# Joining the quadrant matmuls of x into one run per batch, with shared tail banks

## The chip, the cores and the metric

The kernel runs on one core of one Trainium2 chip. Times are device microseconds (us) of one execution. A kernel's time is the median of its runs. All runs were at a granted TensorE clock of 0.998 to 1.000 of full speed.

TensorE (PE) multiplies; its weights are loaded by separate instructions (PEld). VectorE (DVE) and ScalarE (ACT) read the results out of PSUM, in which this kernel keeps eight tiles of 512 float columns; they are called banks here.

## The reference, cut to what matters

```python
# q, k, v: 8 batches, 8 heads, 576 positions, 64 per head
q_s = softmax(q, axis=-1)
k_s = softmax(k, axis=2)                       # over the positions
kv  = einsum('bhsd,bhse->bhde', k_s, v)        # 64 x 64 per head
x   = einsum('bhsd,bhde->bhse', q_s, kv)       # -> 4608 tokens x 512
out = (silu(x @ w_gate) * (x @ w_val)) @ w_out # 512 -> 1536 -> 512
```

Nearly all arithmetic is in the last line. `kv` and `x` are small, but they use only part of the 128x128 array.

## The kernel before: the parts that matter

Each batch is handled in two groups of four heads (`G` is 0 or 1). `kv` has 64 rows and 128 columns of weights; `x` has 64x64, so four matmuls, one on each quadrant of the array, run together. A quadrant run has a first piece of five position tiles (320 columns) and a tail of four (256 columns), because a bank holds 512 float columns.

```python
BANKS = ((0, 5), (5, 9))

def x(b, G, piece, eng=nc.scalar):
    s = st[b, G]
    t0, t1 = piece
    n = 64 * (t1 - t0)
    xp = [f_tile("xp") for _ in range(2)]            # two banks, one for each h
    for g in range(2):
        for h in range(2):
            r = slice(64 * h, 64 * h + 64)
            nc.tensor.matmul(
                out=xp[h][64 * g:64 * g + 64, 0:n].rearrange("p (t c) -> p t c", c=64),
                lhsT=s["kn"][r, g, :], rhs=s["qt"][g][r, t0:t1, :],
                start=True, stop=True)
    c0 = b * S + 64 * t0
    copy(eng, xt[:, 2 * G, c0:c0 + n], xp[0][:, 0:n])
    nc.vector.tensor_copy(out=xt[:, 2 * G + 1, c0:c0 + n], in_=xp[1][:, 0:n])

def x_both(b, G, eng=nc.scalar):
    for piece in BANKS:
        x(b, G, piece, eng)
    st.pop((b, G))

def kv_pair(b):                                      # both groups: 36 matmuls, 4 banks
    kv(b, 0)
    kv(b, 1)
    for G in range(NG):
        kn_recip(b, G)
        kn(b, G, 1, nc.vector)
        kn(b, G, 0, nc.vector)
# ... (cut)
for ci, (c0, n) in enumerate(chunks):                # 448 tokens, then 512 each
    b = ci + 2
    # ... (cut)
    if ci == 0:
        steps = {2: lambda: kv_kn(2, 0, True), 4: lambda: x_both(2, 0),
                 7: lambda: kv_kn(2, 1, True), 10: lambda: x_both(2, 1)}
    elif b < B:
        steps = {8: lambda: kv_pair(b), 9: lambda: x_both(b, 0),
                 10: lambda: x_both(b, 1)}
    for m in range(MT):                              # 12 "rows" of 128 hidden units
        # ... (cut: at rows 3 and 7 the exponentials of batch b and the w_out matmuls)
        m_unit(c0, n, m)                             # g_ps, u_ps: 8 full-array matmuls
        if m in steps:
            steps[m]()
```

A *row* below is one `m_unit`: four matmuls into `g_ps`, four into `u_ps`, then the SiLU on ACT and the product on DVE, which read the two banks. A *round* is one set of `kv` or `x` matmuls that run together: four quadrants for `x`, two halves for `kv`. A *visit* is an unbroken run of rounds between full-array matmuls. `kn` is `kv` after normalisation, written back as the weights of `x`. A *chunk* is the 448 or 512 tokens that twelve rows work on. `f_tile` hands out the eight PSUM banks in turn; a bank comes free when its last reader is done.

The softmax here doesn't subtract the row's maximum and nothing guards it: scores larger than these inputs give would overflow.

Of the kernel before, what the change touches and what calls it, by code (L numbers as in the profile page):

```python
# [15 lines left out]
def kernel(  # L16
# [19 lines left out]
    nc = tc.nc  # L36

    B, H, S, D = q.shape
# [6 lines left out]
    NG = H // 4  # L45
# [10 lines left out]
    def f_tile(name):  # L56
        return psp.tile([128, 512], FP32, tag="ps", name=name)
# [4 lines left out]
    xt = const.tile([128, KT, n_tok], BF16, name="xt", tag="xt")  # L62
# [39 lines left out]
    def copy(eng, out, in_):  # L102
        if eng is nc.scalar:
            nc.scalar.copy(out=out, in_=in_)  # L104
        else:
            eng.tensor_copy(out=out, in_=in_)  # L106


    st = {}
    BANKS = ((0, 5), (5, 9))  # L110

    def exp(b, G, what):
        s = st.setdefault((b, G), {"vb": vbs[G]})
        s["e" + what] = at.tile([128, T, 2, 64], BF16, tag="e" + what, name="e" + what)
        nc.scalar.activation(  # L115
            out=s["e" + what],
            in_=raw[what, b, G].rearrange("p h (t d) -> p t h d", d=64),
            func=AF.Exp,
        )
# [58 lines left out]
    def kv(b, G):  # L178
        s = st[b, G]
        s["kv"] = [f_tile("kv") for _ in range(2)]  # L180
        for t in range(T):
            for g in range(2):
                r = slice(64 * g, 64 * g + 64)
                nc.tensor.matmul(  # L184
                    out=s["kv"][g][:, 0:129],
                    lhsT=s["ek"][r, t, :, :].rearrange("p h d -> p (h d)"),
                    rhs=s["vb"][r, t, 0:129],
                    start=(t == 0),
                    stop=(t == T - 1),
                )  # L190

    def kn_recip(b, G):
        s = st[b, G]
        s["kvr"] = at.tile([128, 2], FP32, tag="kvr", name="kvr")
        for g in (1, 0):
            nc.vector.reciprocal(out=s["kvr"][:, g:g + 1], in_=s["kv"][g][:, 128:129])
# [13 lines left out]
# [4 lines that stand above are left out]
        xp = [f_tile("xp") for _ in range(2)]  # L214
# [5 lines that stand above are left out]
                    lhsT=s["kn"][r, g, :],  # L220
                    rhs=s["qt"][g][r, t0:t1, :],
                    start=True, stop=True,
# [9 lines that stand above are left out]
# [8 lines left out]
    def kv_kn(b, G, split=False):  # L240
        kv(b, G)
        kn_recip(b, G)
        kn(b, G, 1, nc.scalar if split else nc.vector)
        kn(b, G, 0, nc.vector)

    def warm_up(n):
        ps = f_tile("warm_ps")
        for _ in range(n):
            nc.tensor.matmul(  # L249
                out=ps[:, 0:256], lhsT=zero[:, 0:128], rhs=zero, start=True, stop=True  # L250
            )

    def kv_pair(b):
        kv(b, 0)
        kv(b, 1)
# [4 lines that stand above are left out]
# [64 lines left out]


    make_identity(nc, ident)
    A, Z = BANKS
    with tc.manual_schedule():
        for G in range(NG):
            load(0, G, "q", q)  # L330
        for G in range(NG):
            load(0, G, "k", k)
            load(0, G, "v", v)
        warm = const.tile([128, 1], FP32, name="warm", tag="warm")
        nc.vector.memset(warm, 0.0)
        nc.scalar.activation(out=warm, in_=warm, func=AF.Exp)
        zero = const.tile([128, 256], BF16, name="zero", tag="zero")
        nc.vector.memset(zero, 0.0)  # L338
        for vb in vbs:
            nc.vector.memset(vb[:, :, 128:129], 1.0)  # L340

        exp(0, 0, "q")
        exp(0, 1, "q")
        norm_sum(0, 0)
        norm_mul(0, 0, nc.gpsimd)
        norm_sum(0, 1)
        norm_mul(0, 1, nc.vector)
        exp(0, 0, "k")
        cast_v(0, 0, nc.scalar)

        w_dma = []
        for c0, n in ((0, 256), (256, 256), (512, 512), (1024, 512)):
            w_dma.append(w_slice(wg, moe_w_gate, c0, n))
            w_dma.append(w_slice(wv, moe_w_val, c0, n))
        tc.add_manual_dep(w_dma[0].ins, dmas["v", 0, 0].ins.name, SYNC, reason="order of loads")
        for m0 in (0, 4, 8):
            w_dma.append(wo_slice(m0, 4))

        warm_up(WARM[0])
        for G in range(NG):  # L360
            for piece in BANKS:
                tr(0, G, piece, nc.vector)
        exp(0, 1, "k")
        kv(0, 0)
        kn_recip(0, 0)
        kn(0, 0, 1, nc.scalar)
        kn(0, 0, 0, nc.vector)
        cast_v(0, 1, nc.vector, *A)
        cast_v(0, 1, nc.scalar, *Z)
        warm_up(WARM[1])  # L370
        x(0, 0, A)
        x(0, 0, Z)
        kv(0, 1)
        kn_recip(0, 1)
        kn(0, 1, 1, nc.scalar)
        kn(0, 1, 0, nc.vector)
        warm_up(WARM[2])
        x(0, 1, A)
        x(0, 1, Z)

        load(1, 0, "q", q, after=w_dma[-3])
        load(1, 1, "q", q)
        for G in range(NG):
            load(1, G, "k", k)
            load(1, G, "v", v)
        load_group(2, 0)

        for m in range(MT):
            m_unit(0, S, m)

        exp(1, 0, "q")
        exp(1, 1, "q")
        exp(1, 0, "k")
        cast_v(1, 0, nc.gpsimd)
        cast_v(1, 1, nc.gpsimd)
        load_group(2, 1)
        o_unit(0, nc.scalar)
        norm(1, 0)
        o_unit(1, nc.scalar)
        exp(1, 1, "k")  # L400
        norm(1, 1)
        o_unit(2, nc.scalar)
        for piece in BANKS:
            tr(1, 0, piece, nc.vector)
        kv_kn(1, 0, split=True)
        for piece in BANKS:
            tr(1, 1, piece, nc.vector)
        exp(2, 0, "q")

        def between():  # L410
            kv_kn(1, 1, split=True)
            x_both(1, 0, nc.vector)

        finish = o_unit(3, between=between)
        exp(2, 0, "k")
        x_both(1, 1)
        finish()
        norm(2, 0)
        tr_dma(2, 0)
        cast_v(2, 0, nc.gpsimd)  # L420
        cast_v(2, 1, nc.gpsimd)
        exp(2, 1, "q")
        exp(2, 1, "k")

        chunks = [(S, 448)] + [(c, 512) for c in range(1024, n_tok, 512)]
        for ci, (c0, n) in enumerate(chunks):
            b = ci + 2
            first_o = 4 * ci
            final = ci == len(chunks) - 1
            steps = {}  # L430
            if ci == 0:
                steps = {2: lambda: kv_kn(2, 0, True), 4: lambda: x_both(2, 0),
                         7: lambda: kv_kn(2, 1, True), 10: lambda: x_both(2, 1)}
            elif b < B:
                steps = {8: lambda: kv_pair(b), 9: lambda: x_both(b, 0),
                         10: lambda: x_both(b, 1)}
            for m in range(MT):
                if ci == 0 and m == 4:
                    norm_sum(2, 1)
                    norm_mul(2, 1, nc.gpsimd)  # L440
                    tr_dma(2, 1)
                    load_group(3, 0)
                    load_group(3, 1)
                if ci > 0 and m in (3, 7):
                    if b < B:
                        att_head(b, m // 4)
                        if m == 7 and b + 1 < B:
                            load_group(b + 1, 0)
                            load_group(b + 1, 1)
                    o_unit(first_o + (0 if m == 3 else 2))  # L450
                    if not (final and m == 7):
                        o_unit(first_o + (1 if m == 3 else 3))
                m_unit(c0, n, m)
                if m in steps:
                    steps[m]()
        o_unit(first_o + 3)
        last = n_tok // 128 - 4
        for j in range(last, last + 3):
            o_unit(j)
        o_last(last + 3)  # L460
# [30 lines left out]
```

## Time and profile before

| | before |
|---|---|
| time, median of the first 3 runs (6 in all) | 319.42 us (319.35 us) |
| span of the profiled run | 317.4 us |
| PE busy | 310.4 us |
| PE waits, all | 1.7 us |

From the page of the kernel before: the span, the busy line (us, share of the span, instructions), and the chain of work that ended last.

```profile
span 317.4 us, 5037 instructions
...
PE 310.4 (98%) x1920; PEld 157.1 (50%) x1948; DVE 175.5 (55%) x332; ACT 149.2 (47%) x224; POOL 31.1 (10%) x33
...
PE 82%; DMA 10%; DVE 3%; POOL 2%; ACT 1%; issue 1%; SPq 0%; DVEq 0%; ACTq 0%
```

PE is the chain. A few matmul records are missing (1920 of 1948), which changes no start that is read below. The waits of PE in the kernel before (who waited for whom, us in total, times, longest):

```profile
PE warm_ps L249 <- DVE zero L338: 1.1, 1, 1.1
PE tp L160 <- DVE qs L140: 0.4, 1, 0.4
PE kv L184 <- DVE vb L106: 0.2, 1, 0.2
```

All three belong to the start. The list misses one place: it counts from a matmul's modelled end, and so hides short waits. By single starts, the first four `g_ps` matmuls of chunk 0 come about 0.6 us late in all, while batch 1's x is being read out (the last cast on DVE ends at 54.56 us, the fourth `g_ps` starts at 54.61 us). Apart from these, the feed-forward part shows no wait to take away; what is left is PE's own instruction stream. That stream around batch 3, from the timeline of PE in the kernel before (start us, us, engine, line, operation, tiles, form, count):

```profile
132.96 1.03 PE L270 MATMUL u_ps<-xt,wv 128*128 128x512 bf16 x4
133.92 1.22 PE L184 MATMUL kv<-vb,ek 64*128 64x129 bf16 x36
135.07 1.04 PE L270 MATMUL g_ps<-xt,wg 128*128 128x512 bf16 x4
135.94 1.03 PE L270 MATMUL u_ps<-xt,wv 128*128 128x512 bf16 x3
136.90 0.44 PE L218 MATMUL xp<-qtd,kn 64*64 64x320 bf16 x8
137.27 1.04 PE L270 MATMUL g_ps<-xt,wg 128*128 128x512 bf16 x4
138.15 1.03 PE L270 MATMUL u_ps<-xt,wv 128*128 128x512 bf16 x4
139.10 0.44 PE L218 MATMUL xp<-qtd,kn 64*64 64x320 bf16 x8
139.47 1.04 PE L270 MATMUL g_ps<-xt,wg 128*128 128x512 bf16 x4
```

One must read the starts here. The durations (379 ns for 512 columns) have modelled ends and overlap the next matmul, which starts 216 ns later, so they show no gap anywhere. A row takes 1.73 us undisturbed (eight starts, 216 ns apart). From the `g_ps` at 137.27 to that at 139.47 it takes 2.20 us: the x visit in between costs 0.47 us. The single records of the first visit (start in us, distance to the last matmul start before) split that:

```
136.591         u_ps, full array, 512 columns
136.900  0.309  xp, first of four quadrants, 320 columns (others 3 to 4 ns apart)
137.060  0.150  xp, first of four quadrants, 256 columns
137.271  0.201  g_ps, full array            (0.201 after the last quadrant's start)
137.498  0.227  g_ps, full array
137.714  0.216  g_ps, full array
```

Evictions of x in the kernel before, groups with different shapes kept apart (count, then busy us and mean ns, then idle time before):

```profile
L226 DVE CAST xt<-xp 128x320 bf16<-128x320 f32 x16 | 7.7, 484 | 0.5 <-PE xp L218 0.5
L226 DVE CAST xt<-xp 128x256 bf16<-128x256 f32 x16 | 6.6, 415 | 0.0
L104 ACT CAST xt<-xp 128x320 bf16<-128x320 f32 x15 | 6.4, 425 | 6.6 <-PE xp L218 6.6
L104 ACT CAST xt<-xp 128x256 bf16<-128x256 f32 x15 | 5.7, 378 | 0.0
```

### The profile page before, as it was taken

How to read it: one execution, taken by the hardware profiler on the slowest of the kernel's cores; microseconds unless marked ns; L12 is line 12 of the kernel's file. 1: busy time of each engine (PE TensorE's matmuls, PEld its weight loads, DVE VectorE, ACT ScalarE, POOL GpSimd, SP SyncE). 2: the span in 40 equal slices, each digit the busy share in tenths (PEclk: the TensorE clock that was granted, in tenths of full speed). 3: DMA queues.
4: the chain of work that ended last, by engine and by line, in shares of the span. 5: the costliest groups of instructions: out<-in, count | busy, mean ns of one | idle time of the engine just before them, and what ended most of it. 6: DMA issues, size and time to landing. Idle time of an engine off the chain costs nothing.

```text
span 317.4 us, 5037 instructions
## 1 busy us (share of the span) xinstructions
PE 310.4 (98%) x1920; PEld 157.1 (50%) x1948; DVE 175.5 (55%) x332; ACT 149.2 (47%) x224; POOL 31.1 (10%) x33
## 2 busy tenths in 40 slices
PE   8999999999999999999999999999999999999995
PEld 6777744554445444444444444444444444444444
DVE  2934479964647664774577366746575333333422
ACT  4753387744763475547364547355734122312300
POOL 1930023121100110011001100020000000000000
PEclk9999999999999999999999999999999999999999
DMA  7999999449145905392519440963150213020134
GB/s 269 252 190 206 281 392 393 130 116 367 22 84 153 379 24 103 74 385 94 103 38 355 162 103 1 310 241 64 41 103 2 44 22 67 3 61 5 35 67 99
DMA packets 39176, 46.34 MB, mean 146 GB/s; under 512 B 16368, under 2 KB 22384, under 8 KB 39152
## 3 DMA queue, kind: packets, MB, share of 16 engines
q1 hardware_dynamic: 33104, 41.17, 42.5%
q0 software_dynamic: 5808, 4.72, 9.7%
q8 instruction: 15, 0.25, 0.3%
q10 hardware_dynamic: 240, 0.13, 0.2%
q14 instruction: 9, 0.07, 0.1%
HBM read 37.75 MB, written 9.44 MB: 149 GB/s over the span
## 4 chain that ended last, share of the span: by engine, by line
PE 82%; DMA 10%; DVE 3%; POOL 2%; ACT 1%; issue 1%; SPq 0%; DVEq 0%; ACTq 0%
PE g_ps L270 26%; PE o_ps L297 26%; PE u_ps L270 26%; DMA wo<-in_moe_w_out_dram 5%; PE kv L184 2%; DMA v<-in_v_dram 2%; DMA q<-in_q_dram 2%; PE xp L218 1%; POOL wg L92 1%; POOL wv L92 1%; DVE qs L140 1%; PE o_ps L318 1%; DVE rs L131 1%; DVE xt L226 0%; SPq L77 0%
## 5 line engine op out<-in xcount | busy, mean ns | idle before, releaser
L278 ACT ACTIVATE sg<-g_ps 128x512 bf16<-128x512 f32 (+2 forms) x120 | 64.9, 554 | 132.9 <-PE g_ps L270 126.8
L279 DVE TENSOR_TENSOR hr<-sg,u_ps 128x512 bf16<-128x512 bf16 (+2 forms) x120 | 74.9, 633 | 90.7 <-PE u_ps L270 84.1
L270 PE MATMUL g_ps<-xt,wg 128*128 128x512 bf16 (+2 forms) x469 | 110.3, 358 | 0.7
L270 PE MATMUL u_ps<-xt,wv 128*128 128x512 bf16 (+2 forms) x468 | 109.6, 357 | 0.7
L297 PE MATMUL o_ps<-wo,hr 128*128 128x512 bf16 x415 | 93.3, 379 | 0.3
L270 PEld LDWEIGHTS <-wv 128*128 128x128 bf16 x480 | 46.9, 98 | 46.9 <-issue 0.3
L270 PEld LDWEIGHTS <-wg 128*128 128x128 bf16 x480 | 45.3, 98 | 46.2 <-issue 2.6
L297 PEld LDWEIGHTS <-hr 128*128 128x128 bf16 x420 | 41.0, 98 | 49.1 <-issue 0.2
L106 POOL CAST vb<-v 128x1152 bf16<-128x1152 f32 x14 | 17.8, 1270 | 167.2 <-DMA v<-in_v_dram 115.0
L131 DVE TENSOR_REDUCE rs<-eq 128x18 f32<-128x1152 bf16 x16 | 21.6, 1352 | 21.9 <-ACT eq L115 21.8
L106 DVE COPY o_sb<-o_ps 128x512 f32<-128x512 f32 x32 | 21.1, 686 | 20.6 <-PE o_ps L297 20.6
L140 DVE TENSOR_TENSOR qs<-eq,rr 128x1152 bf16<-128x1152 bf16 x14 | 19.8, 1415 | 0.5
L115 ACT ACTIVATE eq<-q 128x1152 bf16<-128x1152 f32 x16 | 18.5, 1163 | 3.2 <-DMA q<-in_q_dram 3.1
L115 ACT ACTIVATE ek<-k 128x1152 bf16<-128x1152 f32 x16 | 18.4, 1152 | 1.3 <-DMA k<-in_k_dram 1.3
L278 ACT ACT_TABLE_LOAD x12 | 15.4, 1283 | 0.2
L208 DVE TENSOR_SCALAR kn<-kv,kvr 64x64 bf16<-64x64 f32 x52 | 14.7, 283 | 1.3
L115 ACT ACT_TABLE_LOAD x11 | 14.1, 1283 | 0.9 <-DMA q<-in_q_dram 0.7
L104 ACT CAST xt<-xp 128x320 bf16<-128x320 f32 (+1 forms) x30 | 10.5, 402 | 6.6 <-PE xp L218 6.6
L226 DVE CAST xt<-xp 128x320 bf16<-128x320 f32 (+1 forms) x32 | 13.1, 450 | 0.5 <-PE xp L218 0.5
L249 PE MATMUL warm_ps<-zero 128*128 128x256 bf16 x80 | 10.9, 302 | 1.1 <-DVE zero L338 1.1
L184 PE MATMUL kv<-vb,ek 64*128 64x129 bf16 x288 | 10.3, 218 | 0.2 <-DVE vb L106 0.2
L184 PEld LDWEIGHTS <-ek 64*128 64x128 bf16 x288 | 8.4, 94 | 3.9 <-ACT sg L278 2.1
(32 smaller groups left out, 64.5 us busy)
## 6 DMA issues: line engine op xcount, KB each, us to landing
q<-in_q_dram SPq DMA_DIRECT2D x16, 576.0 KB, 7.0
k<-in_k_dram SPq DMA_DIRECT2D x16, 576.0 KB, 8.5
v<-in_v_dram SPq DMA_DIRECT2D x16, 576.0 KB, 9.4
out_dram<-o_sb SPq DMA_DIRECT2D x70, 128.0 KB, 2.4
wo<-in_moe_w_out_dram POOLq DMA_DIRECT2D x3, 512.0 KB, 19.0
wg<-in_moe_w_gate_dram POOLq DMA_DIRECT2D x2, 512.0 KB, 11.3
wv<-in_moe_w_val_dram POOLq DMA_DIRECT2D x2, 512.0 KB, 13.1
wg<-in_moe_w_gate_dram POOLq DMA_DIRECT2D x2, 256.0 KB, 6.0
```

The lines of the kernel that those rows point to most:

```text
L106: eng.tensor_copy(out=out, in_=in_)
L115: nc.scalar.activation(out=s["e" + what], in_=raw[what, b, G].rearrange("p h (t d) -> p t h d", d=64), func=AF.Exp,)
L131: nc.vector.reduce_sum(out=rs, in_=s["eq"].rearrange("p t h d -> p (t h) d"), axis=mybir.AxisListType.X)
L140: eng.tensor_mul(s["qs"].rearrange("p t (h d) -> p (t h) d", d=64), s["eq"].rearrange("p t h d -> p (t h) d"), s["rr"].to_broadcast([128, ...
L184: nc.tensor.matmul(out=s["kv"][g][:, 0:129], lhsT=s["ek"][r, t, :, :].rearrange("p h d -> p (h d)"), rhs=s["vb"][r, t, 0:129], start=(t == 0),
L208: nc.vector.tensor_scalar_mul(out_, src, sc)
L226: nc.vector.tensor_copy(out=xt[:, 2 * G + 1, c0:c0 + n], in_=xp[1][:, 0:n])
L249: nc.tensor.matmul(out=ps[:, 0:256], lhsT=zero[:, 0:128], rhs=zero, start=True, stop=True)
L270: nc.tensor.matmul(out=p_[:, 0:w_], lhsT=w[:, kk, ms], rhs=xt[:, kk, c:c + w_], start=(kk == 0), stop=(kk == KT - 1),)
L278: nc.scalar.activation(out=sg[:, 0:w_], in_=g_ps[:, 0:w_], func=AF.Silu)
L279: nc.vector.tensor_mul(hr[:, m, r:r + w_], sg[:, 0:w_], u_ps[:, 0:w_])
L297: nc.tensor.matmul(out=o_ps, lhsT=hr[:, m, r0:r0 + 128], rhs=wo[:, m, :], start=(m == 0), stop=(m == MT - 1),)
```

## The change

From batch 2 on, both groups' x matmuls run in one visit of 16 after row 10. The two 256-column tails of the groups lie side by side in one bank for each `h`, so that the visit needs six banks instead of eight, and each tail bank is read out by one instruction. Batch 2 gets the schedule of the other batches: one kv visit, one x visit.

```diff
+    def x_pair(b):
+        ps = [[f_tile("xa") for _ in range(2)] for _ in range(NG)]
+        z = [f_tile("xz") for _ in range(2)]
+        (_, n_a), n_z = A, 64 * (Z[1] - Z[0])
+        n_a *= 64
+        c0 = b * S
+        for G in range(NG):
+            s = st.pop((b, G))
+            for t0, t1 in BANKS:
+                for g in range(2):
+                    for h in range(2):
+                        r = slice(64 * h, 64 * h + 64)
+                        o = ps[G][h][:, 0:n_a] if t0 == 0 else z[h][:, G * n_z:(G + 1) * n_z]
+                        nc.tensor.matmul(
+                            out=o[64 * g:64 * g + 64, :].rearrange("p (t c) -> p t c", c=64),
+                            lhsT=s["kn"][r, g, :],
+                            rhs=s["qt"][g][r, t0:t1, :],
+                            start=True, stop=True,
+                        )
+            for h, eng in ((0, nc.scalar), (1, nc.vector)):
+                copy(eng, xt[:, 2 * G + h, c0:c0 + n_a], ps[G][h][:, 0:n_a])
+        for h, eng in ((0, nc.scalar), (1, nc.vector)):
+            copy(
+                eng,
+                xt[:, h:h + 2 * NG - 1:2, c0 + n_a:c0 + S],
+                z[h].rearrange("p (g c) -> p g c", g=NG),
             )
@@ (cut)
-            if ci == 0:
-                steps = {2: lambda: kv_kn(2, 0, True), 4: lambda: x_both(2, 0),
-                         7: lambda: kv_kn(2, 1, True), 10: lambda: x_both(2, 1)}
-            elif b < B:
-                steps = {8: lambda: kv_pair(b), 9: lambda: x_both(b, 0),
-                         10: lambda: x_both(b, 1)}
+            if b < B:
+                steps = {8: lambda: kv_pair(b), 10: lambda: x_pair(b)}
```

More of the change, by code (lines that the diff above doesn't have):

```diff
@@ L109 @@
     st = {}
-    BANKS = ((0, 5), (5, 9))
+    A, Z = BANKS = ((0, 5), (5, 9))
     def exp(b, G, what):
@@ L251, in warm_up @@
             )
+    def x_pair(b):
[24 more added lines that the diff above has]
+                z[h].rearrange("p (g c) -> p g c", g=NG),
+            )
     def kv_pair(b):
@@ L326 @@
     make_identity(nc, ident)
-    A, Z = BANKS
     with tc.manual_schedule():
```

## The prediction

> **What bounds the kernel now.** TensorE's instruction stream. The page gives PE 310.4 us busy of 317.4 us (98%); the chain of waits that ended last is 82% PE, the rest loads in the first 45 us. The list of PE's waits holds 1.7 us in all. In the steady part 512-column matmuls start every 216 ns, so a gap in PE's own stream goes straight into the time.
>
> **Where such gaps are.** Single starts in the timeline (batch 3, near 137 us):
> - The first quadrant matmul of an x visit starts 309 ns after the last 512-column matmul, 93 ns late. The four quadrants start 3 to 4 ns apart; the 256-column four start 150 ns after the 320-column four.
> - The next full-array matmul starts 201 ns after the last quadrant start, though 256 columns need about 107 ns (estimate from 216 ns for 512): some 90 ns late. The second full one is 11 ns late.
> - One x visit (8 matmuls) lengthens the stream by 0.475 us: about 0.27 us streaming (150 plus an estimated 124 ns), 0.20 us for going in and out.
> - A kv visit costs 0.737 us for one group (batch 2), 1.259 us for both (batch 3): joining two saves 0.215 us.
>
> The Trainium skill ("TensorEngine Tiling (Array Packing)", Key Properties) says that changing the tiling mode drains the engine; the 93 and 90 ns agree.
>
> **What the change removes.** The matmuls stay. Batches 3 to 7: two x visits become one, an estimated 0.749 us instead of 0.950, 0.201 us saved each, 1.0 us in all. Batch 2: two kv and two x visits become one of each: 0.215 + 0.203 = 0.42 us. Sum 1.42 us, all on PE's critical stream.
>
> **What it moves, off the path.** Evictions of x fall from eight to six per batch: two 320-column pieces per engine (ACT 425, DVE 485 ns), then one 512-column tail each (estimated 0.6 and 0.69 us) instead of two of 378 and 415 ns. Batch 2's kn moves wholly to DVE: done 2.5 us after kv, as in batch 3 now. The PSUM ring is tighter: six banks at once, four of them kv's, free when kn ends, two feed-forward row 9's, free when DVE's product for it ends. By batch 3's times that is 3.2 us after kv's end; the tail matmuls want them at 3.3 us (batch 2) to 3.7 us (later): no wait, with 0.1 us to spare in batch 2. After batch 2 the next chunk reads the tails at once; DVE should finish about 0.2 us before. Later chunks' first reads touch only 320-column pieces. I expect at most 0.1 to 0.2 us given back.
>
> **Prediction.** 319.42 - 1.42 = 318.0 us; 80% range 317.2 to 318.9 (the before runs alone spread over 1 us). Faster by over 2%: 0.01; within 2%: 0.98; slower by over 2%: 0.01.
>
> **What would show it.** In the timeline: one group of 16 quadrant matmuls per batch, rounds 150, 124 and 150 ns apart, its stretch 0.75 us. PE's waits stay under 2 us, without an entry at the x tiles. x casts of batches 2 to 7: 18 per engine instead of 24. Span shorter by 1.3 to 1.5 us.
>
> **What would make it wrong.** Rounds not following at once, because the second group's weights can't be loaded while earlier rounds run; a wait of the tail matmuls for row 9's product in batch 2; PE stalling at the next chunk's start on the tail casts; or the price being per round of weights, not per visit, which would leave the time as it is.

## The result, and the profile after

| | before | after |
|---|---|---|
| time, median of 6 runs | 319.35 us | 317.81 us |
| lowest, highest | 319.02, 320.06 | 317.44, 318.14 |
| ratio after / before, 95% interval | | 0.9948, 0.9934 to 0.9962 |
| span of the profiled run | 317.4 us | 315.4 us |
| start of the last matmul, counted from the second x visit of batch 1 | 260.58 us | 258.96 us |

A ratio is the mean time of one kernel's runs over that of the other's of the same rounds, so it is not quite the ratio of the medians in the table. The kernel is faster by half a per cent, within the 2% band.

The last row is the most useful measure, and it is worked out from single records of the traces. The beginning (loads of inputs and weights) varies from run to run by some tenths of a us. From the second x visit of batch 1 on, the list shows no wait of PE in either profile, the 0.6 us at the start of chunk 0 are there in both, and the stretch to the last matmul repeats very closely: 258.96 us in one profiled run of the changed kernel and 258.97 us in another. I call it the *PE stretch*. The change takes 1.62 us out of it. The other 0.3 us of the difference in span are start-up: batch 1's second x visit starts at 53.03 us in the trace of before and at 52.70 us in that of after; in the other run of the changed kernel it starts at 53.04 us.

The page of the changed kernel:

```profile
span 315.4 us, 5058 instructions
...
PE 310.0 (98%) x1948; PEld 158.1 (50%) x1948; DVE 176.7 (56%) x330; ACT 147.3 (47%) x214; POOL 30.3 (10%) x33
...
PE 94%; DVE 4%; DMA 1%; ACT 0%; issue 0%
```

PE's busy time hardly moved, since overlapping durations hide the gaps. The larger PE share of the chain says only that the chain runs another way through the start-up (DMA 1% of it instead of 10%). PE's waits in the changed kernel:

```profile
PE warm_ps L249 <- DVE zero L365: 1.1, 1, 1.1
PE tp L160 <- DVE qs L140: 0.4, 1, 0.4
PE kv L184 <- DVE vb L106: 0.2, 1, 0.2
```

They are the same three, with nothing at the new tiles `xa` and `xz`. Single starts bear that out: in all six batches the rounds of the joined visit lie the same 150, 99 to 100 and 125 to 126 ns apart. The timeline of PE around batch 3 in the changed kernel:

```profile
132.89 1.22 PE L184 MATMUL kv<-vb,ek 64*128 64x129 bf16 x36
134.04 1.04 PE L298 MATMUL g_ps<-xt,wg 128*128 128x512 bf16 x4
134.92 1.03 PE L298 MATMUL u_ps<-xt,wv 128*128 128x512 bf16 x4
135.78 1.03 PE L298 MATMUL g_ps<-xt,wg 128*128 128x512 bf16 x4
136.65 1.03 PE L298 MATMUL u_ps<-xt,wv 128*128 128x512 bf16 x4
137.60 0.33 PE L266 MATMUL xa<-qtd,kn 64*64 64x320 bf16 x4
137.76 0.28 PE L266 MATMUL xz<-qtd,kn 64*64 64x256 bf16 x4
137.87 0.31 PE L266 MATMUL xa<-qtd,kn 64*64 64x320 bf16 x4
138.01 0.28 PE L266 MATMUL xz<-qtd,kn 64*64 64x256 bf16 x4
138.22 1.04 PE L298 MATMUL g_ps<-xt,wg 128*128 128x512 bf16 x4
```

There is one visit of 16 instead of two of 8. Its edges are as before: 310 ns at the way in, 201 ns at the way out. Inside, the rounds of four start 150, 99 and 126 ns apart; only the first of them takes the 150 ns. From the `u_ps` before to the `g_ps` after, the single records give 0.926 us. Less the 0.216 us that two full matmuls always lie apart, plus the 0.011 us by which the second `g_ps` comes late, the visit costs 0.721 us. By the same working two visits cost 0.951 us in the kernel before, so each batch saves 0.23 us (0.231 us is used below).

The evictions of x for batches 2 to 7 after the change:

```profile
L106 DVE CAST xt<-xa 128x320 bf16<-128x320 f32 x12 | 5.3, 481 | 0.0
L104 ACT CAST xt<-xa 128x320 bf16<-128x320 f32 x12 | 4.5, 430 | 3.1 <-PE xa L266 3.1
L106 DVE CAST xt<-xz 128x512 bf16<-128x512 f32 x6 | 4.1, 679 | 0.0
L104 ACT CAST xt<-xz 128x512 bf16<-128x512 f32 x6 | 3.6, 607 | 0.0
```

They are 18 per engine instead of 24 (the groups shown for the kernel before count batches 0 and 1 too). One tail of 512 columns takes 607 ns on ACT instead of two of 378 ns.

### The profile page after: what moved, and what is told of

Same layout as the page of the kernel before. It is cut to its first block, busy times and chain, and to the rows that moved or that the text cites. A ratio compares the mean times of both kernels' runs of the same rounds, so it can differ in the third digit from the quotient of the medians.

```text
span 315.4 us, 5058 instructions
## 1 busy us (share of the span) xinstructions
PE 310.0 (98%) x1948; PEld 158.1 (50%) x1948; DVE 176.7 (56%) x330; ACT 147.3 (47%) x214; POOL 30.3 (10%) x33
## 4 chain that ended last, share of the span: by engine, by line
PE 94%; DVE 4%; DMA 1%; ACT 0%; issue 0%
PE g_ps L298 30%; PE u_ps L298 30%; PE o_ps L325 28%; PE kv L184 3%; DMA q<-in_q_dram 1%; PE o_ps L346 1%; DVE rs L131 1%; PE xa L266 1%; DVE qs L140 1%; DVE xt L226 0%; DVE qt L106 0%; PE xz L266 0%; ACT eq L115 0%; DVE kn L208 0%; PE tp L160 0%; PE warm_ps L249 0%
## 5 line engine op out<-in xcount | busy, mean ns | idle before, releaser
L298 PE MATMUL g_ps<-xt,wg 128*128 128x512 bf16 (+2 forms) x480 | 111.6, 358 | 0.2
L298 PE MATMUL u_ps<-xt,wv 128*128 128x512 bf16 (+2 forms) x480 | 111.0, 358 | 0.0
L106 POOL CAST vb<-v 128x1152 bf16<-128x1152 f32 x14 | 17.0, 1216 | 167.9 <-DMA v<-in_v_dram 157.9
L208 DVE TENSOR_SCALAR kn<-kv,kvr 64x64 bf16<-64x64 f32 x56 | 15.9, 283 | 1.3
L249 PEld LDWEIGHTS <-zero 128*128 128x128 bf16 x80 | 8.4, 108 | 2.9 <-DVE zero L365 1.1
L104 ACT CAST xt<-xa 128x320 bf16<-128x320 f32 x12 | 4.5, 430 | 3.1 <-PE xa L266 3.1
```

The source lines that it names most:

```text
L104: nc.scalar.copy(out=out, in_=in_)
L106: eng.tensor_copy(out=out, in_=in_)
L208: nc.vector.tensor_scalar_mul(out_, src, sc)
L249: nc.tensor.matmul(out=ps[:, 0:256], lhsT=zero[:, 0:128], rhs=zero, start=True, stop=True)
L298: nc.tensor.matmul(out=p_[:, 0:w_], lhsT=w[:, kk, ms], rhs=xt[:, kk, c:c + w_], start=(kk == 0), stop=(kk == KT - 1),)
```

## The experiments

**The theory.** PE pays a price each time that its stream goes from full-array matmuls into tiled ones and back, whatever is done inside. The change saves six x visits and one kv visit, 6 x 0.231 + 0.215 = 1.60 us. The shared tail bank does not save time itself; it is what lets the single visit run without waiting for banks.

**The rivals.** (1) The gain comes from fewer and larger evictions. (2) The price is per round of weights, not per visit. (3) Joining is all that counts and the banks are a detail. (4) The lost time belongs to x's operands or shapes, not to the tiling as such; or to tiling by columns alone.

The first four runs shared one chip, on which the kernel before took 319.56 us (median of 11). All kernels here gave correct results.

### The changed kernel again

> The changed kernel itself, on the chip of the next three, so that they can be compared with it as well as with the kernel before. Expected 317.8 us, ratio to before 0.995.

Measured: 317.89 us, ratio 0.9947 (0.9935 to 0.9959). The gain repeats on another chip; the PE stretch is 258.97 us.

### One visit, but every tail in a bank of its own

```diff
-                steps = {8: lambda: kv_pair(b), 10: lambda: x_pair(b)}
+                steps = {8: lambda: kv_pair(b), 10: lambda: (x_both(b, 0), x_both(b, 1))}
```

> One run of 16 quadrant matmuls per batch after row 10 and the joined kv of batch 2 as in the change, but each group's tail in banks of its own, so that the run asks for all eight banks and makes eight evictions. If the price is per visit and the shared tail bank is what lets the run go without a wait: the last round takes the bank of row 10's u_ps, which in the changed kernel's trace is read until 0.45 us after that round would start; with the semaphore about 0.5 us of wait per batch, 3.0 us for six batches, 320.8 us, slower than the kernel before, and PE's waits show the vector engine's product as releaser at xp. If joining the visits is all that counts and the banks are a detail: 317.8 us, as the changed kernel.

Measured: 320.49 us, ratio 1.0032 (1.0019 to 1.0045), slower than before. The PE stretch is 261.77 us, 2.80 us longer than in the changed kernel; the estimate was 3.0. The timeline of all engines in this kernel, batch 3:

```profile
138.57 0.67 PE L218 MATMUL xp<-qtd,kn 64*64 64x320 bf16 x13
138.75 0.69 DVE L307 TENSOR_TENSOR hr<-sg,u_ps 128x512 bf16<-128x512 bf16 x1 [0.49 <-PE u_ps L298]
138.94 1.31 ACT L104 CAST xt<-xp 128x320 bf16<-128x320 f32 x4 [0.53 <-PE xp L218]
139.35 1.54 DVE L226 CAST xt<-xp 128x320 bf16<-128x320 f32 x4
139.42 0.30 PE L218 MATMUL xp<-qtd,kn 64*64 64x256 bf16 x3 [0.18 <-ACT xt L104]
```

And of PE's waits:

```profile
PE xp L218 <- ACT xt L104: 0.9, 5, 0.2
PE xp L218 <- DVE hr L307: 0.2, 1, 0.2
```

Thirteen matmuls run at once, the last three wait. The fourteenth is the first to write the second bank of the last pair, the bank that row 10's `u_ps` had. DVE's product for row 10 reads that bank until about 139.4 us, just when PE goes on. The wait is put down to an ACT cast in five of the six batches, though the expectation named DVE. That cast reads a bank which no matmul of this visit asks for again, and the product ends at the right moment; this is the reading of a wait for several semaphores, and I go by the times. By single starts, the last round is split by 445 to 448 ns in each of the six batches, more than the list's 0.2 us, which again counts from a modelled end. Rival 3 falls: joined without shared tails, the visit loses more than joining saves.

### Shared tails, but two visits

```diff
-                steps = {8: lambda: kv_pair(b), 10: lambda: x_pair(b)}
+                steps = {8: lambda: kv_pair(b), 9: lambda: x_visit(b, 0, (0, 1)),
+                         10: lambda: x_visit(b, 1, (0, 1))}
```

`x_visit(b, G, pieces)` issues the rounds of one group into the same six tiles as the change, and the evictions; the two tail evictions come after the second group.

> The shared tail banks and six evictions of the change and its joined kv of batch 2, but the x matmuls of group 0 after row 9 and those of group 1 after row 10, as before: two visits of 8 matmuls. If the price is per visit: 0.231 us more per batch than the changed kernel, 1.4 us in all, 319.2 us. If the gain came from fewer and larger evictions: 317.8 us, as the changed kernel.

Measured: 319.44 us, ratio 0.9996 (0.9984 to 1.0008). The PE stretch is 260.36 us, 1.39 us longer than in the run of the changed kernel beside it. With all of the change's evictions and banks, but two visits, the gain is gone but for what the joined kv of batch 2 brings (0.2 us in the PE stretch against before). Rival 1 falls.

### Four visits

```diff
+                steps = {8: lambda: kv_pair(b), 9: lambda: x_visit(b, 0, (0,)),
+                         10: lambda: x_visit(b, 1, (0,))}
+                mids = {10: lambda: x_visit(b, 0, (1,)), 11: lambda: x_visit(b, 1, (1,))}
```

`mids` are issued between the `g_ps` and the `u_ps` matmuls of a row.

> The same as the two-visit kernel, but every round of four quadrant matmuls is a visit of its own (after row 9, in the middle of row 10, after row 10, in the middle of row 11): four visits, the same matmuls, evictions and banks. If the price is per visit and linear: three visits more than the changed kernel, 3 x 0.231 x 6 = 4.2 us, 322.0 us, at most 0.2 us more for tails that come later in batch 2. If the price is per round of weights, all of it was there already: 317.8 us.

Measured: 321.93 us, ratio 1.0079 (1.0065 to 1.0092). The PE stretch is 263.13 us, 4.16 us more than in the run of the changed kernel beside it. Per added visit that is 4.16 / 18 = 0.231 us, the same as with two visits. The rounds and their weights are the same in all three kernels, 24 rounds (four in each of six batches), so rival 2 falls. The price is linear in the number of visits:

| x visits per batch | time | PE stretch | added per added visit |
|---|---|---|---|
| 1 (the change) | 317.89 us | 258.97 us | |
| 2 | 319.44 us | 260.36 us | 0.232 us |
| 4 | 321.93 us | 263.13 us | 0.231 us |

### The price by itself: 28 added visits

These four kernels are the changed kernel with something added after rows 0, 1, 4 and 5 of chunks 1 to 7. They multiply zeros into banks that nobody reads. The control adds one full-array matmul:

```diff
+    def extra():
+        ps = [f_tile("ex") for _ in range(2)]
+        nc.tensor.matmul(
+            out=ps[0][:, 0:128], lhsT=zero[:, 0:128], rhs=zero[:, 0:128], start=True, stop=True
+        )
@@ (cut)
+                if ci > 0 and m in (0, 1, 4, 5):
+                    extra()
```

The other three replace the one matmul by four quadrants, by two halves of the rows, or by two halves of the columns, each moving the same 128 columns at the same time. In the quadrant kernel:

```diff
+        for g in range(2):
+            for h in range(2):
+                r = slice(64 * h, 64 * h + 64)
+                nc.tensor.matmul(
+                    out=ps[h][64 * g:64 * g + 64, 0:128], lhsT=zero[r, 0:64],
+                    rhs=zero[r, 0:128], start=True, stop=True,
+                )
```

> The changed kernel with 28 extra visits (after rows 0, 1, 4 and 5 of chunks 1 to 7), each one full-array matmul of zeros, 128 columns, into a bank that nobody reads. It is the control: no change of tiling mode. Expected 28 x about 0.056 us = 1.6 us more than the changed kernel, 319.4 us, whatever theory holds.

> The same 28 extra visits, each four 64x64 quadrant matmuls of 128 columns that run together, so that they stream as long as the control's one. If going in and out of a tiling mode costs about 0.2 us: 28 x 0.25 = 7.0 us more than the changed kernel, 324.8 us. If the lost time at the edges of x is a matter of its operands, its waits or its shape (320 and 256 columns) and not of the visit: near the control, 319.4 us.

> The same 28 visits, each two matmuls of 64 rows by 128 columns of the array that run together, 128 columns moved: tiling by rows only. If every change of tiling mode costs the same: 324.8 us, as the quadrants. If the price comes from splitting the columns of the array[...]: near the control, 319.4 us.

> The same 28 visits, each two matmuls of 128 rows by 64 columns of the array that run together: tiling by columns only. If every change of tiling mode costs the same: 324.8 us. If the price comes from splitting the rows: near the control, 319.4 us.

The rival about columns rests on the Trainium skill, "TensorEngine Tiling (Array Packing)", Restrictions, which says that column tiling disables the fast weight load. No run here shows which loads were fast ones; one load took 98 ns on the full array, 92 to 93 ns on row halves and 106 ns on column halves. Measured on one chip, where the kernel before took 319.41 us (median of 7):

| added visit | time | ratio to before | stream longer per visit | less the control |
|---|---|---|---|---|
| full array (control) | 319.36 us | 0.9996 (0.9980 to 1.0013) | 0.056 us | |
| four quadrants | 326.02 us | 1.0206 (1.0190 to 1.0223) | 0.287 us | 0.231 us |
| two row halves | 325.80 us | 1.0195 (1.0180 to 1.0211) | 0.269 us | 0.213 us |
| two column halves | 325.92 us | 1.0198 (1.0182 to 1.0213) | 0.283 us | 0.227 us |

The fourth column is from single starts, as for the x visit above: from the matmul before to the full matmul after, less 216 ns, with the 11 ns of the second full matmul after tiled visits. It varies by a few ns over the 28. The medians agree: (326.02 - 319.36) / 28 = 0.238 us. I had expected about 0.2 us for the quadrants, and 324.8 us; at 28 visits the missing 0.03 us become 1 us. Rival 4 falls: zeros, without waits, of another shape, pay the same, and tiling by rows alone pays nearly all of it.

The timeline of PE, first of the control, then of the quadrant kernel:

```profile
108.04 1.03 PE L304 MATMUL u_ps<-xt,wv 128*128 128x512 bf16 x4
108.90 0.22 PE L283 MATMUL ex<-zero 128*128 128x128 bf16 x1
108.96 1.03 PE L304 MATMUL g_ps<-xt,wg 128*128 128x512 bf16 x4
```

```profile
109.58 1.03 PE L308 MATMUL u_ps<-xt,wv 128*128 128x512 bf16 x4
110.54 0.25 PE L286 MATMUL ex<-zero 64*64 64x128 bf16 x4
110.72 1.04 PE L308 MATMUL g_ps<-xt,wg 128*128 128x512 bf16 x4
```

Four `u_ps` take 0.864 us of the stream. In the control `ex` starts 0.86 us after the first of them and `g_ps` 0.06 us later. In the quadrant kernel these are 0.96 and 0.18 us.

The weight loads show more. In the control the weights of `ex` start loading 2 ns after the start of the matmul before, a whole matmul ahead. The Trainium skill ("TensorE: Matmul & The Clock Gate", Part 2, LDWEIGHTS) describes this pull-ahead. In the quadrant kernel the first weight load starts 308 ns after that matmul and only 2 ns before its own. On the way out the load of `g_ps`'s weights likewise starts only 4 to 5 ns before its matmul. So at a change of tiling the pull-ahead is lost. The price may be the emptying of the array, the weights that load in the open, or both; no run here parts them.

### Batch 2 as it was, the rest changed

```diff
+            if ci == 0:
+                steps = {2: lambda: kv_kn(2, 0, True), 4: lambda: x_both(2, 0),
+                         7: lambda: kv_kn(2, 1, True), 10: lambda: x_both(2, 1)}
+            elif b < B:
```

> The change for batches 3 to 7 only; batch 2 keeps its four visits (kv and x of each group by itself) and its separate tails. If the gain adds up visit by visit: 0.231 for x and 0.215 for kv come back, 0.45 us over the changed kernel, 318.25 us, and PE's stream for batch 2 is 0.45 us longer in the trace. If batch 2's schedule mattered in another way (its kn on the vector engine, its later kv), the difference is not 0.45.

Measured: 318.85 us (318.00 to 318.89), ratio 0.9964 (0.9950 to 0.9978). This interval meets that of the changed kernel, so the times alone are inconclusive. The PE stretch is 259.47 us, 0.50 us over the changed kernel (258.97 us) against 0.45 expected. Of that, 0.06 us is a later start of one x visit, the first of batch 2 (345 instead of 283 ns after the matmul before it). Its first matmul waits for the DMA transpose of that group's q, which was issued at 58.81 us and landed at 62.135 us; the matmul was due at 62.114 us and started at 62.176 us. In the kernel before, the same DMA landed at 62.382 us, 0.055 us before the visit, which started undelayed. PE's list of waits doesn't show this one. The rest of the 0.50 us is the two extra visits.

### The tail evictions twice

```diff
-        for h, eng in ((0, nc.scalar), (1, nc.vector)):
+        for h, eng in 2 * ((0, nc.scalar), (1, nc.vector)):      # the two tails only
             copy(
                 eng,
                 xt[:, h:h + 2 * NG - 1:2, c0 + n_a:c0 + S],
```

> The changed kernel with each tail eviction made twice (the same data written again): 0.61 us more on the scalar and 0.68 us more on the vector engine per batch. If evictions of x are off the critical path: 317.8 us, at most some 0.6 us more in all at the one place where the tails are read at once (start of chunk 1). If they are on it: 6 x 0.65 = 3.9 us more, 321.7 us.

Measured: 318.54 us, ratio 0.9965 (0.9952 to 0.9979), beside the last kernel on a chip where the kernel before took 319.74 us. The PE stretch is 0.63 us longer than in the changed kernel, and all but 0.02 us of it lies between batch 2's x visit and batch 3's kv visit, where chunk 1 begins. The timeline there of this kernel, cut to the lines that matter:

```profile
72.63 1.22 ACT L104 CAST xt<-xz 128x512 bf16<-128x512 f32 x2
73.13 1.41 DVE L106 CAST xt<-xz 128x512 bf16<-128x512 f32 x2
...
73.90 0.38 PE L298 MATMUL g_ps<-xt,wg 128*128 128x512 bf16 x1
...
74.59 0.81 PE L298 MATMUL g_ps<-xt,wg 128*128 128x512 bf16 x3 [0.31 <-DVE xt L106]
```

The same moment in the changed kernel:

```profile
73.21 0.68 DVE L106 CAST xt<-xz 128x512 bf16<-128x512 f32 x1
...
73.83 1.03 PE L298 MATMUL g_ps<-xt,wg 128*128 128x512 bf16 x4
```

In the changed kernel DVE ends the tail at 73.89 us, and the second `g_ps` matmul, the first that reads what DVE wrote, is due at 73.83 + 0.216 = 74.05 us. There are 0.16 us to spare, once; doubling the tails uses them up there (and holds up the first `g_ps` too, which starts at 73.90 us, after ACT's second tail ends at 73.85 us) and costs nothing in the five later batches. From batch 2 on evictions of x are off the critical path, but in batch 2 not by much.

## Why the prediction was right

It gave 318.0 us with a range of 317.2 to 318.9; 317.81 us was measured.

- *PE's own stream bounds the kernel, and gaps in it go straight into the time.* Right. The PE stretch follows the number of visits, and PE's listed waits are the same three before and after.
- *A visit costs 0.20 us for going in and out, whatever it does.* Right in kind, shown by two, four and 28 added visits. The size was 0.231 us (0.201 forecast). The term mis-sized is the streaming of the second group's rounds: the prediction added 150 + 124 = 0.274 us for them, where the stream grew by 0.245 us. I had taken 150 ns for every 320-column round, but that value holds only for the first round of a visit; the later one takes 126 ns, and the 256-column round before it 99 ns. The other 24 ns of the first round thus recur with every visit and belong to its price.
- *The sum of 1.42 us.* The stream gained 1.62 us. Six times the 0.03 us above is 0.18 us of the difference.
- *Joining batch 2's two kv visits saves 0.215 us.* Right: 1.48 us for two before (0.737 and 0.738), 1.26 us for the joined one after.
- *Evictions are off the path; 18 casts instead of 24 per engine.* Right, by the two-visit kernel and by the doubled tails.
- *Banks free in time, with 0.1 us to spare in batch 2; the tails ready 0.2 us before chunk 1.* Right. In the changed kernel DVE's product for row 9 of that chunk ends at 71.71 us and the tail matmul that needs its bank starts at 71.86 us; the tails are ready 0.16 us early. Nothing was given back.
- *Span shorter by 1.3 to 1.5 us; rounds 150, 124 and 150 ns apart; stretch 0.75 us.* Somewhat off. The span was 2.0 us shorter, 1.62 us of it from the stream and the rest from start-up that also varies between two runs of the same kernel. The rounds were 150, 99 and 126 ns apart, the stretch 0.721 us.

Joining batch 1's visits was not tried: the feed-forward rows that follow read all of its x at once, so its evictions would have nothing to hide behind. That is argued, not shown; the traces show only that they hold up the first rows by about 0.6 us as it is.

## What to carry to other kernels

Where PE's stream is the bound, count how often it changes its tiling, and read the price from starts of single matmuls, not from busy time, which hides it. Small matmuls of one tiling belong together, but only as far as the PSUM banks for the whole run are free when it starts: here, after row 10, the joined run paid only because the tails shared banks; no other place for it was tried. An edit worth half a per cent can be settled if a stretch of the trace is found that repeats to a hundredth of a us, and if the suspected price is multiplied. A list of waits that rests on modelled ends can miss short ones; single starts show them.

## What the Trainium skill lacked or had wrong

- "TensorEngine Tiling (Array Packing)", Key Properties, says that a change of tiling mode drains the engine. These traces show time lost at each change, which fits a drain without proving one; the page gives no price. Here going in and out cost 0.231 us for quadrants, 0.227 us for column halves and 0.213 us for row halves, at a granted clock of 0.999 to 1.000.
- The page's sentence on the drain covers a change between two tiled modes as well, again without a price. One place here shows that it pays too: in batch 1 of the kernel before, the first quadrant matmul of x starts 145 ns after the last kv matmul, where kv's own rounds lie 53 to 64 ns apart.
- "TensorE: Matmul & The Clock Gate", Part 2, tells that weight loads are pulled ahead of running matmuls, names two conditions for it (row groups without conflict, or the background weight buffer), and does not tell that it stops at a change of tiling. Here the load started 2 ns after the start of the matmul before in the control, and 308 ns after it at the edge of the quadrants.
- The tiling page's advice to read several tiles of one bank with one instruction ("PSUM Bottleneck") held in time of the engine (607 ns on ACT for one tail of 512 columns, 378 ns for each of two of 256), but it brought nothing to the kernel's time here. What the shared bank brought was a bank: without it the joined visit waited about 0.45 us in each of six batches.
